# Three buffers instead of two in the ring of 2 KB tiles for output copies and decoder scratch

## Chip, cores and metric

The kernel runs on one core of one Trainium2 chip. The metric is the device time of one execution in microseconds (us); the time given for a version is the median of its runs. A trace of one execution, taken by the hardware profiler, stands beside it; times inside the trace count from the start of its span.

## What is computed

Two parts follow each other: an attention with a window of 32 positions on either side and 32 global positions, and a gated product with two dense layers.

```python
def _attn_ref(q_l, k_l, v_l, q_g, k_g, v_g):     # 8 batches, 8 heads, 512 local and 32 global positions, 64 per head
    s_g = scale * np.matmul(q_g, k_all.transpose(0, 1, 3, 2))
    out_g = np.matmul(sm(s_g), v_all)
    ...
    s_ll = np.where(mask, s_ll, -1000000000.0)   # |i - j| <= 32
    s_l = np.concatenate([s_lg, s_ll], axis=-1)
    out_l = np.matmul(sm(s_l), np.concatenate([v_g, v_l], axis=2))
    return np.concatenate([out_g, out_l], axis=2)

def _moe_ref(x, w_val, conv_w, w_out):           # x: 8 x 544 x 512, from the attention
    for k in range(K):                           # K = 5
        gate_pre += conv_w[k][None, None, :] * xp[:, k:k + S, :]
    gate = 1.0 / (1.0 + np.exp(-gate_pre))
    val = x @ w_val
    return gate * val @ w_out
```

## The kernel before

The attention goes in 32 units `u`: a batch (8) and a pair of heads (4). Of a unit, TensorE (PE) makes the scores (`s`), VectorE (DVE) adds the mask and takes row maxima (`mx`), ScalarE (ACT) takes exponentials (`exp`), PE transposes them in two halves (`t28.0` is half 0 of unit 28), ACT or DVE copies these out of PSUM (`tc`), PE multiplies with the values (`av`), DVE normalizes (`eps`, `norm`), PE transposes again (`xt`). The global rows of a batch go a like way (`gs`, `gmax`, `gexp`, `gt`, `gtc`, `gav`). Then the five taps of the convolution run on DVE (`tap`, `conv`), ACT makes the gate (`sig`), and each operand of the dense layers is split into a high and a low part (`xh`, `xl`).

The dense part of batch `b` has two stages of four groups with twelve matmuls each: `g1.b.e` (line 646), whose result DVE multiplies with the gate (`gv`) and which is split again (`gh`, `gl`); and `g2.b.r` (line 674), whose result, 128 rows of the output, is copied from PSUM into an SBUF tile with a factor of 0.5. This copy is `ob.b.r`, by ACT (line 322) or DVE (line 234, the line of a helper that every operation of DVE and GpSimd shares); the tile's tag is `ob`, allocated in line 678. ACT then issues the store of its 256 KB into the result (`st.b.r`, line 855). There are 32 such copies and stores; the two of the global rows (`obg`) take tiles of the same ring.

The tag `ob` is a ring of 2 KB per partition and tile. Before the outputs, the decoding of the eight weight blocks takes its scratch from the same ring (`wa`, line 378; steps `w0.s0` to `w7.s7`). A tile of the ring is free for its next taker when the last reader of the one before is done; for an output copy that reader is its store, so the copy waits for the store's landing.

The order of all engines' work is a table of step names, `ORDER` (lines 52 to 158). `name:ACT` sets a step's engine, `name@5` its PSUM bank. `Plan.order` walks through the table and emits each step where it stands; what `plan.ring` notes (line 266 for `ob`) is not read there. So a ring's size sets addresses and waits, not the order. Around the step on which the prediction turns the table reads (lines 132 to 135):

```text
conv27.0 conv27.1 g2.4.2.3 ob.4.2:ACT st.4.2 sig26 iv28 conv27.2 conv27.3 g2.4.3.0@2 t28.1@1 tc28.1:ACT g2.4.3.1
g2.4.3.2 g2.4.3.3 ob.4.3:ACT st.4.3 g1.5.0.0@3 g1.5.0.1 gs7@64 gmax7.0 s29@01 mx29.0 gmax7.1 exp29.0 mx29.1 exp29.1
t28.0@2 tc28.0:DVE g1.5.0.2 g1.5.0.3 gv.5.0 g1.5.1.0@6 gexp7.0 g1.5.1.1 g1.5.1.2 g1.5.1.3 gv.5.1 t29.1@0 tc29.1:DVE
t29.0@5 gh.5.0:DVE tc29.0:ACT av28@6 eps28:DVE norm28 av29@0 eps29:DVE gt7.0@2 xt28@4 g1.5.2.0@5 norm29 xc28:ACT
```

`g2.4.3` and `t28.0` share PSUM bank 2, so `t28.0` follows the copy `ob.4.3`. `iv28` is SyncE's issue of the last load, the values of unit 28 (line 347); each load is held back until PE's last step ahead of it in the table is done. In batch 0 the like pair is `ob.0.2` (its bank is 4) and `t10.0@4`.

Of the kernel before, what the change touches and what calls it, by code (L numbers as in the profile page):

```python
# [10 lines left out]
F32 = mybir.dt.float32  # L11
F32R = mybir.dt.float32r
I32 = mybir.dt.int32
# [7 lines left out]
DM = H * D  # L21
KW = 5
P = 128
# [218 lines left out]
def attention_moe(ctx, tc, qk, vw, maskd, w_val, w_out, out):  # L242
# [4 lines left out]
    sb = ctx.enter_context(tc.tile_pool(name="sb", bufs=2))  # L247
    ps = ctx.enter_context(tc.tile_pool(name="ps", bufs=1, space=PSUM))

    plan = Plan()  # L250
# [12 lines left out]
    plan.ring("xh", NX, ["zr"], ["zr"])  # L263
    plan.ring("g", 1, ["w"])
    plan.ring("gv", 2, ["zf"], ["zf"])
    plan.ring("ob", 2)

    small = cp.tile([P, 2 * P + NDT * KW * 2], I32, name="small")
    mask = small[:, :2 * P].bitcast(mybir.dt.bfloat16).rearrange("p (i c) -> p i c", i=4)
# [48 lines left out]
    def scale(name, out, in_, by):  # L318

        eng = plan.tasks[name].eng  # L320
        if eng == "ACT":
            A.activation(out=out, in_=in_, func=AF.Copy, scale=by)  # L322
        else:
            (V if eng == "DVE" else G).tensor_scalar(out=out, in0=in_, scalar1=by, scalar2=None, op0=ALU.mult)

    def copy(name, out, in_):
        eng = plan.tasks[name].eng
        if eng == "ACT":
            A.copy(out, in_)  # L329
        else:  # L330
            (V if eng == "DVE" else G).tensor_copy(out, in_)
# [12 lines left out]
    def transfer(out, in_):  # L344


        ins = nc.sync.dma_start(out, in_).ins
        if last_pe:
            tc.add_manual_dep(ins, last_pe[0].name, after, reason="a load's place in the line")
# [4 lines left out]
    def weight(k):  # L354
        of_val = k < NDT
        c = k % NDT
        src = w_val if of_val else w_out
        whi, wlo = (wvh, wvl) if of_val else (woh, wol)
        hi_t, lo_t = whi[:, c, :], wlo[:, c, :]
        box = {}  # L360

        def load():
            if of_val:
                if c % 2 == 0:
                    wraws["pair"] = sb.tile([P, 2, 2 * DM], I32, tag=("gh", "gl")[c // 2], name=f"wraw{k}", bufs=1)
                raw = wraws["pair"][:, c % 2]
            else:
                raw = sb.tile([P, 2 * DM], I32, tag="pm", name=f"wraw{k}", bufs=4)
            if of_val:
                transfer(raw.rearrange("p (t n) -> p t n", t=NDT),  # L370
                         src[:, c * P:c * P + P].bitcast(I32).rearrange("(t p) n -> p t n", p=P))
            else:
                transfer(raw, src[c * P:c * P + P, :].bitcast(I32))
            box["raw"] = raw

        def step(n):
            if n == 0:
                box["a"] = sb.tile([P, DM], I32, tag="ob", name=f"wa{k}", bufs=2)
                raw = box["raw"].rearrange("p (n two) -> p n two", two=2)
                box["steps"] = f64_parts(raw, box["a"], lo_t, lambda n: plan.tasks[f"w{k}.s{n}"].eng)  # L380
            box["steps"][n]()

        def high():
            copy(f"w{k}.high", hi_t, box["a"].bitcast(F32))

        wraws[k] = load
        for n in range(8):
            plan.add(f"w{k}.s{n}", ("DVE", "ACT") if n == 0 else "DVE", lambda n=n: step(n), [f"w{k}.s{n - 1}" if n else f"wl{k}"],
                     take=[] if n else [("ob", f"w{k}")], lock=True)
        plan.add(f"w{k}.high", ("ACT", "DVE", "POOL"), high, [f"w{k}.s3"], lock=True)  # L390
        plan.add(f"w{k}", "FREE", lambda: None, [f"w{k}.high", f"w{k}.s7"],
                 give=[("ob", f"w{k}")] + ([] if of_val else [("pm", f"w{k}")]))
# [243 lines left out]
    def moe(key, n, x0, deps_x, deps_gate, before, store):  # L636

        box = {}
# [36 lines left out]
                         stop=(e == NDT - 1 and q == 2)))  # L675

        def ob(r):
            box["ob", r] = sb.tile([P, DM], F32, tag="ob", name=f"ob{key}_{r}", bufs=2)
            if (key, r) == ("g", n // P - 1):
                A.activation(out=box["ob", r][:, :DM // 2], in_=box["po", r][:, :DM // 2], func=AF.Copy, scale=0.5)  # L680
                V.tensor_scalar(out=box["ob", r][:, DM // 2:], in0=box["po", r][:, DM // 2:], scalar1=0.5, scalar2=None, op0=ALU.mult)
            else:
                scale(f"ob.{key}.{r}", box["ob", r], box["po", r], 0.5)

        for e in range(NDT):
            for t in range(NDT):
                name = f"g1.{key}.{e}.{t}"
# [19 lines left out]
        for r in range(n // P):  # L707
            for e in range(NDT):
                name = f"g2.{key}.{r}.{e}"
                plan.add(name, "PE", lambda r=r, e=e: g2(r, e),  # L710
                         [last, f"gl.{key}.{e}", f"w{NDT + e}"], take=[("bank", name[:-2])] if e == 0 else [],
                         give=[("g", key)] if (r, e) == (n // P - 1, NDT - 1) else [])
                last = name
            plan.add(f"ob.{key}.{r}", "ACT" if (key, r) == ("g", n // P - 1) else ("ACT", "DVE"), lambda r=r: ob(r), [last], take=[("ob", name[3:-2])],
                     give=[("bank", name[:-2])])
            plan.add(f"st.{key}.{r}", "ACT", lambda r=r: store(r, box["ob", r]), [f"ob.{key}.{r}"])
            plan.add(f"sd.{key}.{r}", "DMA", lambda: None, [f"st.{key}.{r}"], give=[("ob", f"{key}.{r}")])
# [260 lines left out]
```

## Time and profile before

| | us |
|---|---|
| median of three runs | 363.26 |
| lowest and highest run | 361.88, 363.44 |
| span of the profiled execution | 360.9 |
| PE busy in it | 349.5 (97%) |
| DVE busy | 307.2 (85%) |
| ACT busy | 233.6 (65%) |
| GpSimd busy | 10.4 (3%) |
| HBM read and written | 56.74 MB, 8.91 MB |

The span runs from the first to the last instruction of the program; a run's time has in it what lies around the span. Of the profiled execution itself only the span is known, not a time. A busy share is an average over the span: matmuls overlap in their pipeline, so PE's 97% does not say that its array works at its peak, and what a wait costs is read at its place.

### The profile page before, as it was taken

To read this page: it belongs to the slowest core of one execution; us is meant where nothing else is said; L and a number is where in the kernel's file an instruction comes from. 1 tells how busy PE (TensorE), PEld (TensorE's weight loads), DVE (VectorE), ACT (ScalarE), POOL (GpSimd) and SP (SyncE) were. 2 spreads that over 40 slices of the span, in tenths; PEclk is the share of its full clock that TensorE was granted. 3 is DMA by queue.
4 is the path that set the end of the run, shared out by engine and by line. 5 is a ranking of instruction groups with operands and counts; after the bars stand their busy time and mean duration, and the time that the engine had idled before them with its cause. 6 is when DMAs were issued, how large, how long until landed. Compare 5 with 4: busy or idle time off the path is not lost.

```text
span 360.9 us, 14693 instructions
## 1 busy us (share of the span) xinstructions
PE 349.5 (97%) x6339; PEld 282.1 (78%) x6339; DVE 307.2 (85%) x1027; ACT 233.6 (65%) x587; POOL 10.4 (3%) x23
## 2 busy tenths in 40 slices
PE   8889999999999999999999999999969999999995
PEld 4566688877888888888788888888758888888894
DVE  4889999999999999999999998987966779894541
ACT  3987999996989798594767276756643934314011
POOL 4300100000000000000000000000000000000000
PEclk9999999999999999999999999999989999999999
DMA  8997566838496349608557474335820012010212
GB/s 298 396 399 293 177 272 256 370 127 344 121 348 281 113 177 319 248 14 308 189 181 307 139 322 146 107 143 181 289 96 3 4 39 81 0 58 35 83 59 58
DMA packets 17104, 66.59 MB, mean 185 GB/s; under 512 B 1808, under 2 KB 3984, under 8 KB 17040
## 3 DMA queue, kind: packets, MB, share of 16 engines
q1 hardware_dynamic: 12240, 57.01, 42.6%
q10 hardware_dynamic: 4800, 8.65, 6.4%
q8 instruction: 49, 0.80, 0.9%
q14 instruction: 15, 0.12, 0.1%
HBM read 56.74 MB, written 8.91 MB: 182 GB/s over the span
## 4 chain that ended last, share of the span: by engine, by line
PE 82%; DMA 7%; DVE 6%; ACT 2%; issue 1%; SPq 1%; DVEq 0%; ACTq 0%
PE psum L646 26%; PE psum L674 20%; PE psum L522 8%; PE psum L533 8%; PE psum L497 7%; DMA out_dram<-ob 4%; PE psum L552 4%; DMA v<-in_vw_dram 3%; PE psum L462 2%; PE psum L618 2%; PE psum L442 2%; PE psum L423 1%; DVE gate L234 1%; DVE pm L234 1%; PE psum L444 1%
## 5 line engine op out<-in xcount | busy, mean ns | idle before, releaser
L234 DVE SCALAR_TENSOR_TENSOR gate<-xc,cw,gate 128x512 f32<-128x512 f32 x120 | 87.6, 749 | 4.8 <-ACT xc L329 2.6
L516 ACT ACTIVATE pm<-pm,mx 128x128 f32<-128x128 f32 x256 | 80.8, 393 | 11.8 <-DVE mx L234 11.2
L234 DVE CUSTOM_DVE_ANT_0 pm<-psum,small 128x128 f32<-128x128 f32 x256 | 57.3, 287 | 4.7 <-PE psum L497 4.7
L646 PE MATMUL psum<-xh,wvh 128*128 128x512 f32 x128 | 53.0, 414 | 0.0
L674 PE MATMUL psum<-woh,gh 128*128 128x512 f32 x128 | 52.3, 408 | 0.0
L646 PE MATMUL psum<-xl,wvh 128*128 128x512 f32 x128 | 50.9, 397 | 0.0
L646 PE MATMUL psum<-xh,wvl 128*128 128x512 f32 x128 | 50.5, 394 | 0.0
L674 PE MATMUL psum<-woh,gl 128*128 128x512 f32 x128 | 50.2, 392 | 0.0
L674 PE MATMUL psum<-wol,gh 128*128 128x512 f32 x128 | 50.0, 390 | 0.0
L522 PE MATMUL psum<-ident,pm 128*128 128x128 f32 x256 | 39.2, 281 | 3.5 <-ACT ob L322 3.1
L522 PEld LDWEIGHTS psum<-ident,pm 128*128 128x128 f32 x256 | 29.5, 142 | 12.0 <-ACT ob L322 4.0
L322 ACT ACTIVATE ob<-psum 128x512 f32<-128x512 f32 x26 | 15.4, 592 | 36.3 <-PE psum L674 23.2
L497 PE MATMUL psum<-qk 64*32 64x128 f32 x2048 | 36.8, 276 | 0.9 <-issue 0.9
L329 ACT COPY pts<-psum 128x512 f32<-128x512 f32 x54 | 30.5, 583 | 9.8 <-PE psum L522 9.4
L497 PEld LDWEIGHTS psum<-qk 64*32 64x32 f32 x2048 | 29.4, 107 | 8.7 <-issue 5.2
L533 PE MATMUL psum<-v,pts 128*32 128x65 f32 x2048 | 35.0, 221 | 1.2 <-DMA v<-in_vw_dram 0.7
L533 PEld LDWEIGHTS psum<-v,pts 128*32 128x32 f32 x2048 | 30.5, 109 | 7.1 <-issue 4.6
L234 DVE SCALAR_TENSOR_TENSOR gv<-gate,psum 128x512 f32<-128x512 f32 x32 | 21.5, 683 | 10.8 <-PE psum L646 10.7
L630 ACT ACTIVATE gate<-gate 128x512 f32<-128x512 f32 x32 | 20.0, 629 | 13.5 <-DVE gate L234 12.9
L646 PEld LDWEIGHTS psum<-xh,wvl 128*128 128x128 f32 x128 | 24.3, 190 | 5.6
L646 PEld LDWEIGHTS psum<-xh,wvh 128*128 128x128 f32 x128 | 24.5, 192 | 4.9 <-DVE gm L234 0.4
L674 PEld LDWEIGHTS psum<-woh,gl 128*128 128x128 f32 x128 | 24.0, 188 | 5.3
(116 smaller groups left out, 542.4 us busy)
## 6 DMA issues: line engine op xcount, KB each, us to landing
v<-in_vw_dram SPq DMA_DIRECT2D x32, 975.0 KB, 7.2
qk<-in_qk_dram SPq DMA_DIRECT2D x32, 624.0 KB, 7.3
out_dram<-ob ACTq DMA_DIRECT2D x32, 256.0 KB, 2.6
wraw<-in_w_val_dram SPq DMA_DIRECT2D x4, 512.0 KB, 12.5
wraw<-in_w_out_dram SPq DMA_DIRECT2D x4, 512.0 KB, 8.5
out_dram<-obg SPq DMA_DIRECT2D x4, 64.0 KB, 1.7
out_dram<-obg ACTq DMA_DIRECT2D x4, 64.0 KB, 2.0
small<-in_mask_dram SPq DMA_DIRECT2D x1, 148.0 KB, 3.9
```

The lines of the kernel that those rows point to most:

```text
L234: ins = made(*args, **kwargs)
L322: A.activation(out=out, in_=in_, func=AF.Copy, scale=by)
L329: A.copy(out, in_)
L442: on_pe(T.transpose(pt[:96, 1 + a, :], pg[:, 96 * a:96 * a + 96], ident))
L497: on_pe(T.matmul((sx, sy)[h][32 * j:32 * j + 32, i, :], qkt[rows, 32 * m:32 * m + 32], qkt[rows, k0:k0 + P], start=True, stop=True))
L516: A.activation(out=pm[:, h, i, :], in_=pm[:, h, i, :], func=AF.Exp, bias=mx[:, c:c + 1], scale=-1.0)
L522: on_pe(T.transpose(pt[:, i, :], pm[:, h, i, :], ident))
L533: on_pe(T.matmul(ax[32 * j:32 * j + 32, h, E1 * i:E1 * i + E1], pts[:, h, i, 32 * j:32 * j + 32], vt[:, block_win(4 * i + j), h, :], start ...
L552: on_pe(T.matmul(xt[:, P * i:P * i + P], xs[:, i].rearrange("p h d -> p (h d)"), ident, start=(i == 0 or u not in XP), stop=(u not in XP), ...
L630: A.activation(out=g, in_=g, func=AF.Tanh, scale=0.5)
L646: on_pe(T.matmul(box["pv", e], w[:, e, t * P:t * P + P], x, start=(t == 0 and q == 0), stop=(t == NDT - 1 and q == 2)))
L674: on_pe(T.matmul(box["po", r], g[:, e, rs], w[:, e, :], start=(e == 0 and q == 0), stop=(e == NDT - 1 and q == 2)))
```

## The change

The ring has three tiles instead of two. The first of the three lines is the table's note, the second the decoder's scratch, the third the output copies.

```diff
-    plan.ring("ob", 2)
+    plan.ring("ob", 3)
...
-                box["a"] = sb.tile([P, DM], I32, tag="ob", name=f"wa{k}", bufs=2)
+                box["a"] = sb.tile([P, DM], I32, tag="ob", name=f"wa{k}", bufs=3)
...
-            box["ob", r] = sb.tile([P, DM], F32, tag="ob", name=f"ob{key}_{r}", bufs=2)
+            box["ob", r] = sb.tile([P, DM], F32, tag="ob", name=f"ob{key}_{r}", bufs=3)
```

On every engine and on SyncE's queue the same instructions stand in the same order. What differs are the semaphores that they wait for. On ACT, at the end of batch 4 (`ob_1` to `ob_3` are the tiles of `ob.4.1` to `ob.4.3`; a `DMAHW` semaphore is raised when a DMA has landed, the others when an engine has done a step):

```order
-L855 DMA out_dram<-ob_1_4818 128x512
+L855 DMA out_dram<-ob_1_4818 128x512 [waits DMAHW2_49]
-L322 ACTIVATE ob_2_4841<-psum 128x512 [waits DMAHW7_49,PE_49]
+L322 ACTIVATE ob_2_4841<-psum 128x512 [waits PE_49]
 L855 DMA out_dram<-ob_2_4841 128x512 [waits DMAHW3_49,Activation_49]
 L630 ACTIVATE gate_4521<-gate_4521 128x512 [waits DVE_49]
 L329 COPY pts_4627<-psum 128x512 [waits PE_49]
-L322 ACTIVATE ob_3_4866<-psum 128x512 [waits DMAHW2_49,PE_49]
+L322 ACTIVATE ob_3_4866<-psum 128x512 [waits DMAHW7_49,PE_49]
 L855 DMA out_dram<-ob_3_4866 128x512 [waits DMAHW4_49,Activation_49]
 L516 ACTIVATE pm_4927<-pm_4927,mx_4928 128x128 [waits DVE_49] x8
```

`DMAHW7` is the landing of `st.4.0`: in a ring of two the copy `ob.4.2` waited for it, in a ring of three `ob.4.3` does. `ob.4.3` no longer waits for `DMAHW2`, the landing of `st.4.1`. On ACT in batch 0 (`ob_2` is the tile of `ob.0.2`):

```order
 L322 ACTIVATE gate_1768<-xc_1706,cw 128x512 [waits Activation_49]
 L329 CAST xh_1770<-xc_1706 128x512
 L449 COPY pgt_0_1779<-psum 96x384 [waits PE_49]
 L450 COPY pgt_0_1779<-psum 128x256 [waits PE_49]
-L322 ACTIVATE ob_2_1807<-psum 128x512 [waits DMAHW2_49]
+L322 ACTIVATE ob_2_1807<-psum 128x512
 L449 COPY pgt_1_1809<-psum 96x384 [waits PE_49,Activation_49]
 L450 COPY pgt_1_1809<-psum 128x256 [waits PE_49]
```

Here the wait for the landing of `st.0.0` falls away, and none takes its place: the third tile was last used by the decoder.

## Rows read from the trace of the kernel before

**Rows 1.** The page's head and its busy times by engine
```profile
span 360.9 us, 14693 instructions
...
PE 349.5 (97%) x6339; PEld 282.1 (78%) x6339; DVE 307.2 (85%) x1027; ACT 233.6 (65%) x587; POOL 10.4 (3%) x23
```
**Rows 2.** Waits, ACT's and PE's: total us, times, longest us
```profile
ACT ob L322 <- DMA out_dram<-ob: 12.1, 3, 6.2
...
PE psum L522 <- ACT ob L322: 3.1, 1, 3.1
```
**Rows 3.** Timeline of ACT: start, duration, line, operation, tiles [idle before <-releaser]
```profile
252.31 0.34 ACTq L855 DMA_DIRECT2D out_dram<-ob  x1
...
260.89 0.57 ACT L329 COPY pts<-psum 128x512 f32<-128x512 f32 x1
...
265.25 0.60 ACT L322 ACTIVATE ob<-psum 128x512 f32<-128x512 f32 x1 [3.79 <-DMA out_dram<-ob]
...
266.26 2.45 ACT L516 ACTIVATE pm<-pm,mx 128x128 f32<-128x128 f32 x8 [0.42 <-DVE mx L234]
```
**Rows 4.** DMA issues at 256.55, 252.31 and 265.88 (st.4.1, st.4.0, st.4.3): KB, us to landing
```profile
out_dram<-ob ACTq DMA_DIRECT2D x1, 256.0 KB, 8.3
...
out_dram<-ob ACTq DMA_DIRECT2D x1, 256.0 KB, 3.2
...
out_dram<-ob ACTq DMA_DIRECT2D x1, 256.0 KB, 2.0
```
**Rows 5.** Windows: length, busy PE, PEld, DVE, ACT, POOL, clock, DMA share, GB/s
```profile
259.00:262.80 3.80, 3.80 (x104) 2.62 (x103) 3.62 (x6) 1.10 (x2) 0.00 (x0) 1.00 0.87 298
...
265.90:269.30 3.40, 3.40 (x10) 2.89 (x11) 1.39 (x9) 3.04 (x9) 0.00 (x0) 0.51 0.21 80
```
**Rows 6.** Chain that ended last, 256 to 272 us: start, duration, what
```profile
256.55 8.32 DMA out_dram<-ob
...
265.90 1.11 PE psum L522 x4
267.01 5.25 PE psum L646 x18
```
**Rows 7.** The same chain, two pieces at the full clock
```profile
108.59 2.77 PE psum L646 x12
...
128.77 0.59 PE psum L522 x4
```
**Rows 8.** Timeline of DVE, 266 to 275 us
```profile
266.51 0.08 DVE L234 DVE_READ_ACCUMULATOR2_ANT mx<- 128x1 f32 x1
...
272.30 0.69 DVE L234 SCALAR_TENSOR_TENSOR gv<-gate,psum 128x512 f32<-128x512 f32 x1 [2.09 <-PE psum L646]
272.90 0.68 DVE L234 COPY pts<-psum 128x512 f32<-128x512 f32 x1
...
274.25 0.17 DVE L234 TENSOR_SCALAR mx<-psum 128x8 f32<-128x8 f32 x1 [0.33 <-PE psum L533]
```
**Rows 9.** Timeline of PE, 265 to 274 us
```profile
265.90 1.11 PE L522 MATMUL psum<-ident,pm 128*128 128x128 f32 x4 [3.06 <-ACT ob L322]
...
273.06 2.02 PE L533 MATMUL psum<-v,pts 128*32 128x65 f32 x128
```
**Rows 10.** The same chain around 84 to 92 us, and a pair of transposes later
```profile
83.85 6.45 DMA out_dram<-ob
...
90.97 1.09 PE psum L522 x8
...
275.55 0.22 PE psum L444 x2
```
**Rows 11.** Timeline of PE at 90 us
```profile
90.45 0.38 PE L444 MATMUL psum<-ident,pg 128*128 128x128 f32 x2
```
**Rows 12.** The load of unit 28, issued at 256.3, and all loads of v: min/median/max
```profile
v<-in_vw_dram SPq DMA_DIRECT2D x1, 975.0 KB, 8.4
...
DMA to landing us min/median/max: 4.5/7.2/15.9
```

## Prediction

> **What bounds the kernel now.** I read the busy shares first, then the waits, then the chain that ended last, then the timelines and windows of the one place to which these lead. TensorE (PE) is busy for 349.5 of the span's 360.9 us [rows 1]: nearly all the time is PE's own work, and a change can only win where PE stands still or runs slowly. The list of waits names the tile of the change [rows 2]: ScalarE (ACT) stood idle 12.1 us in three places before an output copy, waiting for the store of an earlier `ob` tile. PE waited for such a copy once, 3.1 us, and no wait in PE's list is longer. So one of ACT's three waits matters, and the question is what it costs and what takes its place.
>
> It is the copy `ob.4.3`. ACT finished the copy before it at 261.46 (260.89 + 0.57), stood idle 3.79 us for a store, and began at 265.25 [rows 3]. That store is `st.4.1`, issued at 256.55 and landed at 264.87 [rows 6]: it took 8.3 us, where one that runs alone takes 2.0 [rows 4]. `ob.4.3` empties PSUM bank 2, into which PE's next step, the transposes `t28.0`, writes. They began at 265.90, after 3.06 us of idle PE [rows 9]; PE had reached them at 262.84. The windows show the second half of the price [rows 5]: in the 3.4 us behind the stop the granted clock was 0.51, the lower of TensorE's two levels (1.2 of 2.4 GHz); before it the clock stood at 1.00.
>
> **The change, part by part.** No instruction is added, removed or moved on any engine or DMA queue; what differs is which landing an output copy or a weight step must wait for.
>
> Weight decoding (`wa`): ACT's and VectorE's (DVE) lists of waits hold none of a `wa` tile for its ring, so nothing is won; 0.
>
> `ob.4.3`: with three tiles it takes the tile of `ob.4.0`, whose store was issued at 252.31 [rows 3] and landed 3.2 us later, at 255.5 [rows 4]. ACT is free at 261.46, and the bank's last matmul lies before the last steps that PE runs up to 262.84 (`g1.5.0.0`, `g1.5.0.1`, `gs7`, `s29`), so the copy runs from 261.46 to about 262.1, ahead of PE's 262.84. The first term is PE's whole idle time, **3.06 us** (265.90 - 262.84).
>
> The clock: from 265.90 the chain gives PE 1.11 us for 4 transposes and 5.25 us for 18 matmuls [rows 6], 6.36 together. At the full clock 4 such transposes take 0.59 and 12 such matmuls 2.77 [rows 7], so 18 take 4.16 and the piece 4.75. The second term is **1.61 us**, given back if PE no longer stops, since the clock was full up to the stop. PE would then be 4.67 us earlier at the end of this piece.
>
> What is late next: DVE did not wait for that copy. It worked on alone until the last row maximum, 266.51 to 266.60 [rows 8], and that stays. Then it copies `tc28.0` and runs `gv.5.0` and `gv.5.1`; such steps follow each other at 0.60 us (272.30 to 272.90 [rows 8]), so `gv.5.1` can start at 267.80, where a shift of 4.67 would want 267.63. PE needs it for bank 6 before `av28`, which began at 273.06 [rows 9], 0.76 us after `gv.5.1`: it now begins at 268.56 and not at 268.39, so **0.17 us** goes back. From there the engines are locked to PE as before: `eps28` on DVE waited for PE by 0.33 us at 274.25 [rows 8], and DVE, free at about 269.4, again meets it with some 0.3 us to spare. ACT lies further inside. The rest of the program moves as one piece.
>
> `ob.0.2`: ACT waited 2.1 us (12.1 less 3.8 and 6.2 [rows 2]) for a store of 6.45 us [rows 10]. PE needed bank 4 from this copy for `t10.0`. The two transposes before began at 90.45 [rows 11] and such a pair takes 0.22 [rows 10]; `t10.0` could have begun at 90.67 and began at 90.97. Removing the wait gives at most 0.30 us; at least 0, if DVE, with 85% of the span [rows 1], takes it back. I take **0.2**, nearer to the upper end because the chain goes on in PE alone behind it.
>
> The third wait, ACT's longest at 6.2 us, has no counterpart among PE's waits [rows 2]: PE's work hides it, so 0. If a later change sped PE up there, this copy would be the next in line, but the third tile frees it too.
>
> Sum: 3.06 + 1.61 - 0.17 + 0.2 = **4.7 us**. The profiled execution spans 360.9 us, so the new span is 356.2. No time of that execution itself is given; the median of the runs, 363.26, lies 2.4 us over its span, and I take the same difference: **358.6 us**. About 0.5% (1.8 us) is what a measurement of this kernel can tell from no change.
>
> **Rivals.** First, the stop moves on by 5 us instead of going away. `t29.1`, which PE reached at 272.26 (267.01 + 5.25 [rows 6]), would be due at 267.59 and needs four exponentials of ACT. They follow DVE's maxima, the last of which ends at 266.60 [rows 8]; at 0.31 us each (2.45 for eight [rows 3]) and run behind each maximum, they end near 267.2, just in time. If they run as now, eight in one block of 2.45 us from 266.26 to 268.71, PE idles 1.1 us and 3.6 us are left of the gain: 359.7. For it speaks the margin of some 0.4 us; against it, that ACT does them in one block now because it was held up itself.
>
> Second, no change: the wait belongs to the profiled execution and the timed runs hardly have it. The row says that the store took 8.3 us beside a load of 975 KB that was issued just ahead of it and took 8.4 [rows 4, 12]. In the Trainium skill, "DMA: Bandwidth & Descriptors", section "Queues, rings and completion order", each DMA engine takes turns between the queues that have work, packet by packet. By that rule a store that has half the engines' time would take about twice its undisturbed time, landing near 260.6, before ACT wants it, and the sum would fall to about 0.2 (363.1). The trace disagrees: this store took four times as long. For the rival: a landing 3.4 us sooner, at 261.46 and not at 264.87, would have left no wait to remove. Against it: the store of 6.45 us in another stage [rows 10] shows the same slowness wherever loads run, and what follows from the program's order recurs in each run. 363.1 us.
>
> Third, slower: the last load of `v`, for unit 28, becomes what `av28` waits for. It lands at 264.7 (issued 256.3, 8.4 us [rows 12]), and now `st.4.3` is issued some 3.8 us sooner, into the same DMA engines. PE will want the load at 268.4. It decides when it lands after 271.6: PE then idles over 3.2 us and, if the clock falls again (1.61), more than 4.8 us is lost. At the longest landing of such a load in this trace, 15.9 us [rows 12], it comes at 272.2, PE idles 3.8, and the time is 363.26 - 4.7 + 3.8 + 1.6 = 364.0. Against it: the store's 256 KB at the 298 GB/s of that stretch [rows 5] cost the load 0.9 us, which puts it at 265.6, with 2.8 us in hand. That the change does not do what it says is excluded by the order of the instructions shown ahead: `ob.4.3` now waits for the landing that `ob.4.2` waited for before.
>
> **How the numbers follow.** The forecast, 358.6, gets 0.78; the stop that moves on (359.7) 0.10; no change (363.1) 0.08; slower (364.0, half of it past 365.1 with a still later load) 0.04. The low end is the sum with all of the 0.30 (4.8 us, 358.5) less the 1.4 us by which the lowest run lies under the median: 357.1. The high end is the first rival with 1.3 us for the same scatter on the other side: 361.0. Between them lie the forecast and nearly all of the first rival. Faster by over 0.5% means below 361.4: 0.78 and 0.10, less 0.01 for runs that scatter, 0.87. Within 0.5%: 0.08, that 0.01 and half of the slower rival, 0.11. Slower by over 0.5%, above 365.1: 0.02.
>
> **What would show it.** In the profile after, `ob.4.3` starts about 261.5 (earlier by what `ob.0.2` gives) with no idle time of ACT put down to a store; the granted clock stays at 1.00 from 260 to 270; `av28` begins near 268.4; PE's busy time falls by about 1.6 us and the span by 4.7. ACT's three waits for stores are gone, the one of 6.2 us replaced by one for PE. I am wrong if PE shows a new idle stretch of over 1 us between 262 and 275 (the row names ACT, DVE or the load), or if the span falls by less than 3 us although the stop at 265.90 is gone.

## The result and the profile after

| | before | after |
|---|---|---|
| median of five runs, us | 363.44 | 359.33 |
| lowest and highest | 361.88, 364.55 | 357.76, 359.64 |
| ratio, 95% interval | | 0.9886 (0.985 to 0.9923) |

The kernel is faster by 1.14%, about 4.1 us (363.44 x 0.0114; 2.8 to 5.5 by the interval). In this document medians hold all runs, while ratios and counts leave out those more than 1.5% above the fastest of their kernel: 7 of the 84 runs of the kernel before, all seven with a mean granted clock below 0.9965 (a mark used further on), and one run of the experiment with `ob.0.2` alone. The page of the profile after, head, busy times, granted clock by slices and the chain that ended last by engine:

```profile
span 357.5 us, 14686 instructions
...
PE 347.6 (97%) x6339; PEld 281.0 (79%) x6339; DVE 307.0 (86%) x1027; ACT 233.6 (65%) x587; POOL 10.4 (3%) x23
...
PEclk9999999999999999999999999999999999999999
...
PE 94%; DMA 2%; DVE 1%; issue 1%; ACT 0%; SPq 0%; DVEq 0%
```

PE is busy for 1.9 us less than before [rows 1] with the same instructions; the span is 3.4 us shorter. The waits after, ACT's and PE's (total us, times, longest):

```profile
ACT ob L322 <- PE psum L674: 23.2, 7, 6.2
...
ACT ob L322 <- DVE gateg L234: 5.1, 1, 5.1
...
PE psum L497 <- issue: 1.5, 1, 1.5
PE psum L745 <- DVE zero L234: 1.4, 1, 1.4
PE psum L497 <- DMA qk<-in_qk_dram: 0.9, 1, 0.9
PE psum L552 <- DVE xs L234: 0.9, 1, 0.9
```

ACT's wait for stores, 12.1 us in three places [rows 2], is gone; its waits before output copies are now for PE or DVE (a copy in the place of the 6.2 us wait now waits 5.1 us for DVE). PE's wait for `ob`, 3.1 us [rows 2], is gone too. ACT's and PE's timelines at the place of the change (start, duration, line, operation, idle time before and its releaser):

```profile
262.14 0.57 ACT L329 COPY pts<-psum 128x512 f32<-128x512 f32 x1
262.60 0.60 ACT L322 ACTIVATE ob<-psum 128x512 f32<-128x512 f32 x1
263.24 0.34 ACTq L855 DMA_DIRECT2D out_dram<-ob  x1
265.76 1.28 ACT L516 ACTIVATE pm<-pm,mx 128x128 f32<-128x128 f32 x4 [2.55 <-DVE mx L234]
267.25 1.28 ACT L516 ACTIVATE pm<-pm,mx 128x128 f32<-128x128 f32 x4 [0.21 <-DVE mx L234]
```

```profile
8.04 1.16 PE L497 MATMUL psum<-qk 64*32 64x128 f32 x64 [0.93 <-DMA qk<-in_qk_dram]
...
91.80 0.38 PE L444 MATMUL psum<-ident,pg 128*128 128x128 f32 x2
92.02 1.04 PE L522 MATMUL psum<-ident,pm 128*128 128x128 f32 x8
...
262.96 1.13 PE L497 MATMUL psum<-qk 64*32 64x128 f32 x64
264.02 0.66 PE L522 MATMUL psum<-ident,pm 128*128 128x128 f32 x4
...
268.67 1.04 PE L522 MATMUL psum<-ident,pm 128*128 128x128 f32 x8
269.69 2.02 PE L533 MATMUL psum<-v,pts 128*32 128x65 f32 x128
```

`ob.4.3` starts as soon as ACT is through with the copy before it (262.60; before it stood idle 3.79 us [rows 3]), and PE goes from `s29` into `t28.0` without a stop (before: 3.06 us of idle [rows 9]). In windows (columns as in [rows 5]) the clock stays full where it was at 0.51:

```profile
262.80:265.90 3.10, 3.10 (x98) 2.65 (x81) 3.03 (x10) 0.55 (x2) 0.00 (x0) 1.00 0.75 284
265.90:269.30 3.40, 3.40 (x19) 2.83 (x18) 3.40 (x19) 3.06 (x9) 0.00 (x0) 1.00 0.04 13
```

**A measure that the start does not disturb.** The two executions did not start alike. Two rows of PE in the kernel before:

```profile
5.15 2.73 PE L497 MATMUL psum<-qk 64*32 64x128 f32 x128
...
261.70 1.13 PE L497 MATMUL psum<-qk 64*32 64x128 f32 x64
```

Before, the first scores ran in one piece; after, PE stood 0.93 us in their middle for a load. At the pair of transposes in batch 0 the kernel after is 1.35 us late (91.80 against 90.45 [rows 11]). So spans of two profiled executions can't be subtracted to a microsecond. From here on the stop is measured from the start of `s29` (the last step that PE runs before it) to the start of `av28` (the first step behind the piece with the low clock): 273.06 [rows 9] - 261.70 = 11.36 us before, 269.69 - 262.96 = 6.73 after. The change is worth **4.63 us** there, in these two executions; the prediction's terms for this place make 4.50 (3.06 + 1.61 - 0.17).

### The profile page after: what moved, and what is told of

Its sections match the earlier page's. It is cut to its first block, busy times and chain, and to the rows that moved or that the text cites. A ratio compares the mean times of both kernels' runs of the same rounds, so it can differ in the third digit from the quotient of the medians.

```text
span 357.5 us, 14686 instructions
## 1 busy us (share of the span) xinstructions
PE 347.6 (97%) x6339; PEld 281.0 (79%) x6339; DVE 307.0 (86%) x1027; ACT 233.6 (65%) x587; POOL 10.4 (3%) x23
## 4 chain that ended last, share of the span: by engine, by line
PE 94%; DMA 2%; DVE 1%; issue 1%; ACT 0%; SPq 0%; DVEq 0%
PE psum L646 26%; PE psum L674 26%; PE psum L533 9%; PE psum L522 9%; PE psum L497 9%; PE psum L552 4%; PE psum L462 3%; PE psum L618 2%; DMA wraw<-in_w_val_dram 2%; PE psum L423 2%; PE psum L442 2%; PE psum L444 1%; PE psum L585 1%; PE psum L478 0%; SPq L347 0%
## 5 line engine op out<-in xcount | busy, mean ns | idle before, releaser
L522 PE MATMUL psum<-ident,pm 128*128 128x128 f32 x256 | 38.4, 278 | 0.3 <-ACT pm L516 0.2
L646 PEld LDWEIGHTS psum<-xl,wvh 128*128 128x128 f32 x128 | 24.1, 189 | 4.2
## 6 DMA issues: line engine op xcount, KB each, us to landing
wraw<-in_w_val_dram SPq DMA_DIRECT2D x4, 512.0 KB, 12.1
```

The lines of the kernel that those rows point to most:

```text
L522: on_pe(T.transpose(pt[:, i, :], pm[:, h, i, :], ident))
L646: on_pe(T.matmul(box["pv", e], w[:, e, t * P:t * P + P], x, start=(t == 0 and q == 0), stop=(t == NDT - 1 and q == 2)))
```

## Experiments

They ran in three groups, each on one chip and beside the kernel before, whose medians in the groups were 362.66, 362.78 and 362.69 us. First come `ob.4.3` alone, the wait put back, the six matmuls and the load at `gs7`; then `ob.0.2` alone, the eighteen matmuls and the two repeats; last the load just behind the store. The ratios are those on record; they are not the quotients of the medians, which differ from them by up to 0.4%, so differences of about a microsecond between kernels, above all of different groups, are not shown.

**The one wait, by itself.** Two tiles stay in the ring; `ob.4.3` alone gets a tile of its own.

```diff
-            box["ob", r] = sb.tile([P, DM], F32, tag="ob", name=f"ob{key}_{r}", bufs=2)
+            own = (key, r) == (4, 3)
+            box["ob", r] = sb.tile([P, DM], F32, tag="oz" if own else "ob", name=f"ob{key}_{r}", bufs=1 if own else 2)
```

> The ring keeps two tiles; the copy ob.4.3 alone gets a tile of its own, so that it waits for PE only. If the stop before t28.0 (3.06 us of idle PE and 1.61 us of half clock) is what the third tile removed, TensorE runs through at the full clock, the shift of PE between 260 and 274 us is -4.6 us, and the time is 4.5 us under the kernel before (ratio 0.987 to 0.988), within 0.5 us of the ring of three. If the gain comes from many small waits of the ring, or from where tiles lie, less than 1 us is gained here.

Measured: 359.62 us, ratio 0.9938 (0.9907 to 0.9969). PE's timeline:

```profile
91.83 0.38 PE L444 MATMUL psum<-ident,pg 128*128 128x128 f32 x2
92.57 1.09 PE L522 MATMUL psum<-ident,pm 128*128 128x128 f32 x8 [0.36 <-ACT ob L322]
...
263.29 1.13 PE L497 MATMUL psum<-qk 64*32 64x128 f32 x64
264.35 0.66 PE L522 MATMUL psum<-ident,pm 128*128 128x128 f32 x4
...
270.02 2.02 PE L533 MATMUL psum<-v,pts 128*32 128x65 f32 x128
```

No stop, and 270.02 - 263.29 = 6.73 us, the same as with three tiles. `ob.0.2` still waits here: PE is idle for 0.36 us before `t10.0`. The ratio missed the 0.987 to 0.988 that was expected: the runs gained 2.2 us (362.66 x 0.0062; 1.1 to 3.4 by the interval; 3.0 by the medians), not 4.5. The place behaves as expected; what it costs in an ordinary run was set too high, as the repeats below show.

**The same wait, put back.** Three tiles, the same addresses and waits as in the changed kernel but one: `ob.4.3` waits for the landing of `st.4.1` again, though it does not use that tile.

```diff
-    plan.ring("ob", 2)
+    plan.ring("ob", 3)
...
+            if (key, r) == (4, 3):
+                ins = A.activation(out=box["ob", r], in_=box["po", r], func=AF.Copy, scale=0.5).ins
+                tc.add_manual_dep(ins, box["st", 1].ins.name, after, reason="the wait put back")
+                return
...
-            plan.add(f"st.{key}.{r}", "ACT", lambda r=r: store(r, box["ob", r]), [f"ob.{key}.{r}"])
+            plan.add(f"st.{key}.{r}", "ACT", lambda r=r: box.update({("st", r): store(r, box["ob", r])}), [f"ob.{key}.{r}"])
```

> The ring has three tiles as in the change, all tiles lie where the change puts them, and one wait is put back: ob.4.3 also waits for the landing of st.4.1. If that wait is the cause, the stop is back: PE idle about 3 us before t28.0, the granted clock near 0.5 for 3.4 us, and the time within 0.5 us of the kernel before (ratio 0.998 to 1.001). If the other waits of the ring or the addresses made the gain, the time stays near the change's (ratio 0.988).

Measured: 362.48 us, ratio 0.9989 (0.9957 to 1.0022): the gain is gone. PE's timeline, and the window behind the stop:

```profile
262.47 1.13 PE L497 MATMUL psum<-qk 64*32 64x128 f32 x64
266.24 1.11 PE L522 MATMUL psum<-ident,pm 128*128 128x128 f32 x4 [2.64 <-ACT ob L680]
...
273.27 0.94 PE L533 MATMUL psum<-v,pts 128*32 128x65 f32 x52
```

```profile
265.90:269.30 3.40, 3.06 (x10) 2.58 (x11) 2.12 (x11) 2.98 (x10) 0.00 (x0) 0.50 0.21 80
```

The stop and the low clock are back, and `s29` to `av28` takes 10.80 us. At this place the one wait is the cause: taken away alone, the stretch is as short as with three tiles; put back alone, the stop is there again and the time is the kernel before's within the interval. What the third tile does elsewhere is small but not settled: the median span of the runs with `ob.4.3` alone (357.9 us) is 0.9 above that of the runs with three tiles (357.0), while the runs with the wait put back (360.7) lie where the kernel before lies on the same chip (360.7).

**Both kernels again, unchanged**, to see what of this repeats. There is no diff.

> The kernel before, unchanged, for a second profile of it. The stop before t28.0 is there again. If its length follows from when st.4.1 lands and when PE arrives, a start of the program that is later by x gives a stop that is shorter by up to x, and a short stop leaves the clock at 1.00; if the stop is part of the order alone, it is 3.0 us long again, with the clock at half for 3.4 us.

> The ring of three, unchanged, on the same chip as the others. If the distance to the kernel before depends on whether the clock falls in the stop, the span lies near 357.5 us in all runs with no run at a mean clock of 0.995 by a fall in the middle, and the gain against runs of the kernel before is about 4 us where these show 0.995 or less and about 2 us where they show 0.997 or more.

Measured: two tiles 361.22 us, ratio 0.9997 (0.9957 to 1.0037); three tiles 358.80, ratio 0.9917 (0.9889 to 0.9945). The profiled execution with two tiles was a surprise. PE's timeline and the landing of its `st.4.1`, issued at 257.17 (KB, us to landing):

```profile
262.32 1.13 PE L497 MATMUL psum<-qk 64*32 64x128 f32 x64
264.37 0.66 PE L522 MATMUL psum<-ident,pm 128*128 128x128 f32 x4 [0.92 <-ACT ob L322]
...
269.99 2.02 PE L533 MATMUL psum<-v,pts 128*32 128x65 f32 x128
```

```profile
out_dram<-ob ACTq DMA_DIRECT2D x1, 256.0 KB, 6.2
```

The wait is there, at the same place in the same program, but the store landed after 6.2 us and not 8.3; PE idled 0.92 us and not 3.06, and its clock did not fall (`t28.0` takes 0.66 us, not 1.11). `s29` began 0.62 us later than before (262.32 - 261.70) and the stop was 2.14 shorter, so neither of the two expectations holds: the store itself was quicker. `s29` to `av28` takes 7.67 us: the stop cost 0.94 (7.67 - 6.73) where it had cost 4.63. So its price varies from run to run. The clock shows how often it is high: 3.4 us at half the clock take 0.5% off the mean granted clock of a span, so I count the runs with a mean under 0.9965.

| runs | below 0.9965 |
|---|---|
| two tiles, kernel before, beside all experiments | 34 of 77 |
| two tiles, this repeat | 3 of 8 |
| three tiles, wait put back | 8 of 12 |
| three tiles, both times | 3 of 17 |
| two tiles, `ob.4.3` with its own | 0 of 8 |
| two tiles, `ob.0.2` with its own | 3 of 11 |
| two tiles, six matmuls ahead of `t28.0` | 1 of 12 |
| eighteen matmuls ahead, or the load moved (four kernels) | 3 of 43 |

Of the runs whose kernel has the wait of `ob.4.3` as it was, 48 of 108 are below it; of those whose kernel has no stop there, 6 of 68.

A run can also come below it by a fall elsewhere: the profiled one of the three-tile repeat has its low clock near the start, behind an idle of 1.76 us. The other low runs with three tiles have no profile.

```profile
22.70:26.10 3.40, 3.40 (x54) 2.12 (x56) 1.89 (x15) 3.32 (x10) 0.00 (x0) 0.50 1.02 410
```

It reaches batch 0's pair of transposes only at 93.94 us, spans 359.6 us, and still needs 6.74 from `s29` (264.99) to `av28` (271.73). Of the 77 runs the 34 have a median span of 361.8 us and the other 43 of 359.9; the 17 runs with three tiles have 357.0. By that the third tile is worth about 4.8 us against the runs that lose the clock there or elsewhere, 2.9 against the rest, and 3.8 against the median of all 77 (360.8). The 2.9 is more than the stop cost in the two profiles in which the clock stayed full (0.94 here, 2.39 with `ob.0.2` alone, 9.12 - 6.73), so a part of it may come from the rest of the ring.

**`ob.0.2` alone**: two tiles, and one more for this copy.

```diff
-            box["ob", r] = sb.tile([P, DM], F32, tag="ob", name=f"ob{key}_{r}", bufs=2)
+            own = (key, r) == (0, 2)
+            box["ob", r] = sb.tile([P, DM], F32, tag="oz" if own else "ob", name=f"ob{key}_{r}", bufs=1 if own else 2)
```

> Two tiles as before, but the copy ob.0.2 of batch 0 alone gets a tile of its own. ACT's 2.1 us wait at 88 us is gone. If the sum's term for it is right, PE starts t10.0 up to 0.3 us earlier and the time is the kernel before's within 0.3 us (ratio 0.998 to 1.001), with the stop before t28.0 in place. If this wait matters more than the trace showed, because ACT's lead of 2 us is carried on, 1 us or more is gained.

Measured: 361.21 us, ratio 0.9975 (0.9936 to 1.0013), an interval that includes no change. PE's timeline:

```profile
91.40 0.38 PE L444 MATMUL psum<-ident,pg 128*128 128x128 f32 x2
91.62 1.04 PE L522 MATMUL psum<-ident,pm 128*128 128x128 f32 x8
...
266.32 0.66 PE L522 MATMUL psum<-ident,pm 128*128 128x128 f32 x4 [2.33 <-ACT ob L322]
```

`t10.0` follows the pair at 0.22 us, as in the changed kernel (92.02 - 91.80) and not at 0.52 as before [rows 10, 11]. The time can't show 0.3 us. This run gives another price of the stop instead: PE idle for 2.33 us with the clock staying full, 9.12 us from `s29` (262.85) to `av28` (271.97).

**Work of PE ahead of `t28.0`**, with two tiles: if PE has something else to do while the store is under way, the wait costs less. In the table six matmuls, then all eighteen, are put ahead of it:

```diff
-t28.0@2 tc28.0:DVE g1.5.0.2 g1.5.0.3 gv.5.0 g1.5.1.0@6 gexp7.0 g1.5.1.1 g1.5.1.2 g1.5.1.3 gv.5.1 t29.1@0 tc29.1:DVE
+g1.5.0.2 g1.5.0.3 t28.0@2 tc28.0:DVE gv.5.0 g1.5.1.0@6 gexp7.0 g1.5.1.1 g1.5.1.2 g1.5.1.3 gv.5.1 t29.1@0 tc29.1:DVE
```

```diff
-t28.0@2 tc28.0:DVE g1.5.0.2 g1.5.0.3 gv.5.0 g1.5.1.0@6 gexp7.0 g1.5.1.1 g1.5.1.2 g1.5.1.3 gv.5.1 t29.1@0 tc29.1:DVE
+g1.5.0.2 g1.5.0.3 g1.5.1.0@6 gexp7.0 g1.5.1.1 g1.5.1.2 g1.5.1.3 t28.0@2 tc28.0:DVE gv.5.0 gv.5.1 t29.1@0 tc29.1:DVE
```

> Two tiles as before; in the table, the six matmuls g1.5.0.2 and g1.5.0.3 (0.232 us each) stand ahead of t28.0 and fill 1.4 us of the idle 3.06 us. The stop shrinks to some 1.7 us. If the clock falls because PE stands still for the whole 3 us, it stays at 1.00 and the gain is 1.4 + 1.6 = 3.0 us (ratio 0.992); if it falls after 1.7 us as well, only 1.4 us is gained (ratio 0.996).

> Two tiles as before; in the table all 18 matmuls g1.5.0.2 to g1.5.1.3 stand ahead of t28.0, and on DVE the copy tc28.0 stays ahead of gv.5.0. PE works through the wait (4.2 us of matmuls against a stop of 3 us), the clock stays at 1.00, and only av28 starts later than with three tiles, since its copy tc28.0 and gv.5.1 come 0.9 us later. If the stop of PE and its clock are all that the third tile removed, the gain is 3.5 to 4.5 us of the stage (the run within 1 us of the ring of three). If the third tile also helped elsewhere, the distance to it is over 1 us.

Measured: 361.03 us, ratio 0.9958 (0.9933 to 0.9983), with six; 361.24, ratio 0.9961 (0.9933 to 0.999), with eighteen. One row of PE of each:

```profile
267.10 0.66 PE L522 MATMUL psum<-ident,pm 128*128 128x128 f32 x4 [1.00 <-ACT ob L322]
```

```profile
272.07 2.02 PE L533 MATMUL psum<-v,pts 128*32 128x65 f32 x128 [0.56 <-DVE gv L234]
```

With six the stop shrinks to 1.00 us and the clock stays full. With eighteen PE no longer waits for `ob`, but `tc28.0`, `gv.5.0` and `gv.5.1` on DVE are late for `av28`. From `s29` to `av28` the first takes 7.97 us (271.35 - 263.38), the second 8.13 (272.07 - 263.94). Either is better than the stop at its dearest, neither is as good as 6.73. By time they gain 1.5 and 1.4 us (0.0042 and 0.0039), half of the three-tile repeat's 3.0, and both expectations missed: 3.0 us was expected with the clock staying full, and a time within 1 us of three tiles, where 2.4 us lie between (361.24 - 358.80). The late `av28` explains 1.40 of these (8.13 - 6.73); the rest stays open.

**The load out of the store's way**, with two tiles: `iv28` is issued at `gs7`, some 6 us later.

```diff
-conv27.0 conv27.1 g2.4.2.3 ob.4.2:ACT st.4.2 sig26 iv28 conv27.2 conv27.3 g2.4.3.0@2 t28.1@1 tc28.1:ACT g2.4.3.1
-g2.4.3.2 g2.4.3.3 ob.4.3:ACT st.4.3 g1.5.0.0@3 g1.5.0.1 gs7@64 gmax7.0 s29@01 mx29.0 gmax7.1 exp29.0 mx29.1 exp29.1
+conv27.0 conv27.1 g2.4.2.3 ob.4.2:ACT st.4.2 sig26 conv27.2 conv27.3 g2.4.3.0@2 t28.1@1 tc28.1:ACT g2.4.3.1
+g2.4.3.2 g2.4.3.3 ob.4.3:ACT st.4.3 g1.5.0.0@3 g1.5.0.1 gs7@64 gmax7.0 iv28 s29@01 mx29.0 gmax7.1 exp29.0 mx29.1 exp29.1
```

> Two tiles as before; in the table, the issue of the last load (unit 28) stands behind gs7, some 5 us later, so that st.4.1 has only the load before it beside itself. If the store is slow because of the load issued just ahead of it, it lands near 260.3 us (3.7 us after its issue), before ACT wants the tile at 261.5, the stop is gone, and 4.5 us is gained with two tiles (ratio 0.988). If stores are slow there for another reason, it still lands near 264.9 and nothing is gained. If the load then lands after 268.4, PE waits at av28 instead, and less is gained.

Measured: 360.06 us, ratio 0.9924 (0.9898 to 0.9951). The landing of `st.4.1`, and PE at `av28`:

```profile
out_dram<-ob ACTq DMA_DIRECT2D x1, 256.0 KB, 3.5
```

```profile
271.52 2.02 PE L533 MATMUL psum<-v,pts 128*32 128x65 f32 x128 [1.02 <-DMA v<-in_vw_dram]
```

With only the load before it beside it, issued some 3.7 us ahead, the store takes 3.5 us and there is no stop, though the ring has two tiles. The last load, issued at 264.05, lands 1.02 us too late for `av28`; `s29` to `av28` takes 7.78. This is the third rival's mechanism, brought on by a later load: 1.05 us (7.78 - 6.73).

**The load just behind the store**, with two tiles and with three (the second with the change's three lines besides):

```diff
-conv27.0 conv27.1 g2.4.2.3 ob.4.2:ACT st.4.2 sig26 iv28 conv27.2 conv27.3 g2.4.3.0@2 t28.1@1 tc28.1:ACT g2.4.3.1
+conv27.0 conv27.1 g2.4.2.3 ob.4.2:ACT st.4.2 sig26 conv27.2 conv27.3 g2.4.3.0@2 t28.1@1 tc28.1:ACT g2.4.3.1 iv28
```

> Two tiles as before; the last load is issued behind g2.4.3.1, some 1.7 us later than before and just behind st.4.1 and not ahead of it. If the store is slow because it stands behind that load, st.4.1 lands within 4 us of its issue, the stop before t28.0 is gone, the load lands before av28 wants it (about 7 us after its issue at 258, against 268.4), and the two-tile kernel comes within 0.7 us of the ring of three (ratio 0.989 to 0.993). If the store stays at 6 to 8 us, nothing is gained.

> Three tiles and the same later load. If the third tile and the later load remove the same stop by two ways, the two together are worth no more than one: within 0.5 us of the ring of three (span about 357). If the shorter stores also help elsewhere, or the later load is late for av28, the span is more than 0.5 us lower or higher.

Measured: two tiles 359.77 us, ratio 0.9926 (0.99 to 0.9951); three 359.53, ratio 0.9924 (0.9898 to 0.995). Landings of `st.4.1` (issued at 258.87) and of the load with two tiles, and PE in batch 0:

```profile
out_dram<-ob ACTq DMA_DIRECT2D x1, 256.0 KB, 3.5
...
v<-in_vw_dram SPq DMA_DIRECT2D x1, 975.0 KB, 5.4
```

```profile
91.59 0.38 PE L444 MATMUL psum<-ident,pg 128*128 128x128 f32 x2
93.05 1.09 PE L522 MATMUL psum<-ident,pm 128*128 128x128 f32 x8 [1.08 <-ACT ob L322]
```

The store lands in time, the load too, there is no stop, and `s29` to `av28` takes 6.74 us with two tiles (264.02 to 270.76) and 6.73 with three (263.16 to 269.89). The two gains do not add: both remove the same wait. With three tiles the median span, 357.7 us, is 0.7 and not at most 0.5 from the 357.0 of three tiles alone, which on two chips shows no difference. A store that has landed makes the third tile needless at this place. In batch 0 it isn't: there `ob.0.2` held PE up by 1.08 us in this execution. Of the kernels run, the changed one has the lowest median, but by less than the intervals are wide (ratios of 0.9924 to 0.9926 here and with the load at `gs7`, 0.9886 and 0.9917 for three tiles): moving one load may serve as well as the tile.

## Why the prediction was right, and where its sizes were off

- **`ob.4.3`, 3.06 us of idle PE: right in place and mechanism.** ACT starts the copy at once, PE does not stop. That it is this wait alone, in this stretch, is shown by the tile of its own (6.73 us for `s29` to `av28`, like the change) and by the wait put back (10.80).
- **The clock, 1.61 us: right in this execution.** The window that had 0.51 has 1.00, and the stretch from `s29` to `av28` fell by 4.63 where 4.50 was said.
- **The step that was mis-sized** is the taking of these two terms whole, from one execution, as what each run loses. Four profiles of this wait gave 3.06, 2.64, 2.33 and 0.92 us of idle PE, and the clock fell behind the first two only. The sum of 4.7 is near the dearest case; the medians of the spans give 3.8, the two ratios 4.1 and 3.0 (362.78 x 0.0083), with intervals of 2.8 to 5.5 and 2.0 to 4.0. The first still holds 4.7, the second doesn't.
- **`gv.5.1`, 0.17 us back: right in sign, a third in size.** `av28` begins 1.02 us behind the transposes before it (269.69 - 268.67), before it was 0.96 (273.06 - 272.10, the start of the same eight transposes). DVE's timeline:

```profile
267.76 0.69 DVE L234 COPY pts<-psum 128x512 f32<-128x512 f32 x1
268.36 1.27 DVE L234 SCALAR_TENSOR_TENSOR gv<-gate,psum 128x512 f32<-128x512 f32 x2
...
270.88 0.17 DVE L234 TENSOR_SCALAR mx<-psum 128x8 f32<-128x8 f32 x1 [0.30 <-PE psum L533]
```

  `gv.5.1` follows `tc28.0` and `gv.5.0` without a gap, as the prediction placed it, and `eps28` waits for PE by 0.30, so DVE has met PE again.
- **`ob.0.2`, 0.2 us: the 0.30 was won, less was kept.** `t10.0` follows its pair at 0.22 us and not 0.52. From the pair to `s29` the kernel before takes 171.25 us (261.70 - 90.45), after 171.16 (262.96 - 91.80): 0.09 net. The upper bound of 0.30 was one execution's too: with two tiles that wait held `t10.0` up by 1.24 us more than its pair in the run with the later load (93.05 - 91.59 - 0.22), and from the pair to `s29` that run took 172.43 (264.02 - 91.59), so there it was not given back. In the four executions with three tiles that stretch took 170.85 to 171.20 us, in the seven in which `ob.0.2` shares two 171.25 to 172.43, and with a tile for `ob.0.2` alone 171.45; so the ring seems to give a few tenths there, not by this copy alone.
- **The third wait, 0: right.** From `av28` to the end both kernels take 87.8 us (360.9 - 273.06, 357.5 - 269.69). The 6.2 us wait for a store was replaced by one of 5.1 us for DVE, where the prediction said PE.
- **The span and the time.** A span of 356.2 was said and 357.5 came: the kernel after reached batch 0's pair 1.35 us later. That belongs to no term of the sum: the eight executions with two tiles stand there at 90.45 to 92.50, and the profile before has the earliest of these. Whether the ring's use by the decoder, put at 0, moves the start by less than this spread is not shown. What lies around the span is 1.8 us (359.33 - 357.5, and so in each run), not 2.4; the 2.4 held the 0.5 us or so by which that profiled execution was quicker than the median. These two errors have opposite signs, and 358.6 is within 0.7 us of the median partly for that.
- **The stop that moves on (359.7): did not come.** ACT's exponentials run as two blocks of four behind DVE's maxima, ending with the second at 268.53, and nothing waits before `t29.1`. The block of eight was a result of ACT's own delay: it stands in the profiles with 3.06, 2.64 and 2.33 us of idle PE, and two blocks of four in that with 0.92.
- **No change (363.1): wrong as a whole, but it held the missing part.** The argument against it was that what follows from the program's order recurs in each run. The wait recurs; its length does not. In the repeat with two tiles the store took 2.1 us less, and the stop cost 0.94. The working by which this rival was weighed misread the rule of turns: turns by packet don't give the store half of the engines' time, since it has as many packets as the load, 128, of 2048 bytes and not 7800. By turns from the start the two would end about together, so the 8.3 us did not speak against the rule.
- **Slower (364.0): did not come.** The load landed at 265.4 (257.53 + 7.9) and `st.4.3`, now earlier, did it no harm. The mechanism is real, as the load at `gs7` shows, but it took some 6 us of delay to bring it on.

## What to carry to other kernels

A ring whose tiles are stored is deep enough if the slowest landing comes before its tile is wanted again. Here the landing was slowest for a store issued together with a large load; look for that pair, and either add a tile or part the two. Price a stop by two fixed steps of the engine that bounds, one ahead and one behind, rather than by the span, and in several executions: the stop's length and the clock behind it are the part that varies most. Work put under a wait helps only until the next engine is late with what was pushed back.

## What the runs showed that was not expected

**A store issued together with a load lands with the load.** With `iv28` issued 0.3 us ahead of `st.4.1`, load and store of the changed kernel took

```profile
v<-in_vw_dram SPq DMA_DIRECT2D x1, 975.0 KB, 7.9
out_dram<-ob ACTq DMA_DIRECT2D x1, 256.0 KB, 7.8
```

In all nine executions with this order the store landed 0.2 to 0.5 us behind the load, which took 6.1 to 8.4 us, although it has a quarter of the load's bytes; with the load issued some 1.5 us behind it, the store took 3.5 and 3.8. In the Trainium skill, "DMA: Bandwidth & Descriptors", section "Queues, rings and completion order", each engine takes turns between queues packet by packet. In the trace each of the two DMAs has 128 data packets, of 7800 and of 2048 bytes, so by turns they would end about together, but the store would be moving all the while. In one place the trace agrees: with the load at `gs7`, `st.4.3` is issued at 264.02 and the load at 264.05, they take 7.2 and 7.3 us, and from 266 to 268 us the loads' queue (q1) and the stores' (q10) moved packets in like number (packets, MB, share of the engines):

```profile
q1 hardware_dynamic: 73, 0.57, 68.1%
q10 hardware_dynamic: 74, 0.15, 19.9%
```

Behind a load that was issued 0.3 us sooner it is not so. In the kernel before, in the 3 us from the issue of `st.4.1` (256.55 to 259.55), the loads' queue was the only one of the two that moved:

```profile
q1 hardware_dynamic: 95, 0.62, 81.0%
```

In all nine executions at most 6 of the store's 128 packets moved in the first 3 us, and in the kernel before its tenth followed the 93rd of the load's. What holds them back is not shown. Why the same load takes 6.1 us in one execution and 8.4 in another stays open: in the repeat with two tiles 343 GB/s moved from 260.00 to 262.80, before 298 from 259.00 to 262.80 [rows 5].

**The clock does not fall behind each stop.** Behind idle stretches of PE of 3.06 and 2.64 us the granted clock was 0.51 and 0.50; behind 2.33 and 0.92 us at the same place it stayed at 1.00; and near the start of one run it was 0.50 behind an idle stretch of 1.76. What decides it was not tried.

**The start varies as much as the change is worth.** By batch 0's pair of transposes the executions profiled stood at 90.45 (before) to 93.94 us (the repeat with three tiles), with the same order of work up to there. From `av28` to the end all twelve took 87.8 or 87.9 us. So what blurs a median of few runs is the start and the stop, not the end.
